# Turning token rows through DRAM and VectorE's 32x32 transposition instead of TensorE, and longer rests in one gating group

## The chip, the cores and the metric

The kernel runs on one core of one Trainium2 chip. The metric is the device time of one execution in microseconds; less is better. A profiled execution also gives a trace, with a span a little shorter than its time.

## The reference

Sliding-window attention feeds a dense feed-forward layer, and that a mixture of eight experts, of which each token uses two:

```python
# attention: 4 batches, 8 heads, 576 positions, head size 64, window 64
mask = (rel >= 0) & (rel < window)
out = softmax(where(mask, scale * q @ k.T, -1e9)) @ v        # -> x, 2304 tokens x 512
# dense layer
h = maximum(x @ w_in, 0)                                     # 512 -> 2048
x = h * h @ w_out                                            # 2048 -> 512
# mixture
noisy = x @ w_gate + log1p(exp(x @ w_noise)) * noise         # 2304 x 8
top2, top2_w = two largest of each row, softmax over the two
for e in range(8):
    for k in range(2):
        m = top2[:, k] == e
        out[m] += top2_w[m, k, None] * (maximum(x[m] @ w1[e], 0) @ w2[e])   # 512 -> 1024 -> 512
```

All of it is float32. The kernel holds each operand of the large matrix products as a pair (high part, rest), and makes three products out of each.

## The kernel before

The 2304 tokens are worked on in six groups g of 384, three tiles of 128 each. For each group PE makes the dense layer over 16 slices f of the hidden width: L1 (L329) gives a slice of h, L2 (L346) adds it to three PSUM accumulators named o. At a group's end the three tiles are copied into SBUF buffers x2 and written to the DRAM tensor x2d (L375). Three more streams are Python generators, from which a function `filler` takes a step here and there between L1 and L2: the attention of group g + 1, the gating of group g - 1, and later the preparation of the next expert's tokens.

The gating of a group needs the tokens with their 512 features on partitions. Four PE transpositions a tile (L387) put a tile into a PSUM bank named att, ScalarE copies it out as the high part (L390), VectorE subtracts for the rest (L391). Eight matmuls (L396) give the logits; a long chain of small VectorE operations finds the two experts of each token, and small matmuls with the triangle `tri` and with `ones` (L457 to L459) count places. Ahead of these, and of the last one of the gating (L501), stand REST = 4 empty yields, so that filling work lies in between while VectorE ends its chain.

Then come nine expert passes: expert 0 in two (three tiles, two tiles), experts 1 to 7 in one pass each of five tiles, at most 624 tokens. In a pass, f runs over 8 slices of the hidden width. Its L1 runs in two halves of 312 columns, each into one of the two PSUM banks h; ScalarE takes the relu (L582), VectorE the rest h (L583), and then the bank is free. `stage2` loads the two weight tiles st2 of the next expert's slice f by two DMAs of 256 KB on SP (L533, L535), from four buffers, and splits them on ScalarE (L148) and POOL (L149). `prep`, begun at f = 4 of each pass, gathers the next expert's token rows from x2d into gx0 to gx4 by indirect DMA on POOL (L546), turns each tile by four PE transpositions (L564), and copies and subtracts as in the gating (L566, L567). At the end of a pass `finish` gathers the rows of out (gy), adds into buffers y, and scatters them (L552).

The generators only give the order in which the program is written. A list scheduler, which knows costs and dependences, then puts the instructions of each engine into an order of its own, and each engine works strictly in that order. DMAs issued by SP take turns over eight lanes, and each waits for the one eight before it.

Of the kernel before, what the change touches and what calls it, by code (L numbers as in the profile page):

```python
# [8 lines left out]
F32 = mybir.dt.float32  # L9
# [4 lines left out]
AF = mybir.ActivationFunctionType  # L14
OP = mybir.AluOpType
AX = mybir.AxisListType
REST = 4
NREST = 1
P0F = 6
PNF = 4  # L20
LB = 4
QB = 0
KT = 1
# [17 lines left out]
def moe_kernel(ctx, tc, q, k, v, w_in, w_out, wg, wn, noise, w1, w2, out):  # L41
    nc = tc.nc
    B, H, S, D = q.shape
    N, DM = out.shape
    E, _, F2 = w1.shape
    F = w_out.shape[0]
    NCC = DM // 128
# [3 lines left out]
    TG = 384  # L51
    TT = TG // 128
    NG = N // TG
# [6 lines left out]
    CT = -(-CAP // 128)  # L60
# [6 lines left out]
    hw = ctx.enter_context(tc.tile_pool(name="hw", bufs=2))  # L67
    xtp = ctx.enter_context(tc.tile_pool(name="xtp", bufs=2))
    ringa = ctx.enter_context(tc.tile_pool(name="ringa", bufs=2 * NF2))
    att = tc.alloc_tile_pool(name="att", bufs=2, side="right")  # L70
# [4 lines left out]
    dram = ctx.enter_context(tc.tile_pool(name="dram", bufs=1, space=DRAM))  # L75
# [6 lines left out]
    def ps(tag):  # L82
        return psum.tile([128, 512], F32, name=tag, tag=tag, bufs={"o": 3, "h": 2, "att": 3}[tag])
# [37 lines left out]
    def late_consts():  # L121
        nc.gpsimd.iota(iotas, pattern=[[1, 128]], base=0, channel_multiplier=0,
                       allow_small_or_imprecise_dtypes=True)
        nc.gpsimd.iota(pidx, pattern=[[0, 1]], base=0, channel_multiplier=1,
                       allow_small_or_imprecise_dtypes=True)
        nc.gpsimd.memset(ones, 1.0)
        nc.gpsimd.affine_select(out=tri, in_=ones, pattern=[[1, 128]], compare_op=OP.is_gt,
                                fill=0.0, base=0, channel_multiplier=-1)
        nc.gpsimd.memset(base, 0.0)
        nc.gpsimd.memset(cnt, 0.0)  # L130
        nc.gpsimd.memset(table, 0.0)
        wf = stg.tile([128, 512], F32, name="cv", bufs=CVB)[:, :NCC * 2 * E].rearrange("p (c e) -> p c e", c=NCC)
        nc.sync.dma_start(wf[:, :, :E], wg.rearrange("(c p) e -> p c e", p=128))
        nc.sync.dma_start(wf[:, :, E:], wn.rearrange("(c p) e -> p c e", p=128))
        nc.scalar.activation(wgn[:, :, 0], wf, AF.Copy)
        nc.gpsimd.tensor_sub(wgn[:, :, 1], wf, wgn[:, :, 0].bitcast(F32))
        nt = stg.tile([N // 128, 128 * E], F32, name="st", bufs=STB)
        nc.sync.dma_start(nt, noise.rearrange("(t p) e -> t (p e)", p=128))
        pn = ps("att")
        for e in range(E):  # L140
            nc.tensor.transpose(pn[:, e * (N // 128):(e + 1) * (N // 128)],
                                nt.rearrange("t (p e) -> t e p", e=E)[:, e], ident[:N // 128, :N // 128])
        nc.vector.tensor_copy(noi.rearrange("p t e -> p e t"),
                              pn[:, :N // 128 * E].rearrange("p (e t) -> p e t", e=E))
# [231 lines left out]
                x2s[g].append(x2)  # L376


    GAT = {}

    def gating(g):
        gat = GAT["pool"]
        x2T = gat.tile([128, 2, NCC, TG], F32R, name="x2T")
        for t in range(TT):
            pt = ps("att")
            for c in range(NCC):
                nc.tensor.transpose(pt[:, 128 * c:128 * c + 128], x2s[g][t][:, 128 * c:128 * c + 128], ident)  # L387
            tl = slice(128 * t, 128 * t + 128)
            src = pt.rearrange("p (c n) -> p c n", c=NCC)
            nc.scalar.activation(x2T[:, 0, :, tl], src, AF.Copy)  # L390
            nc.vector.tensor_sub(x2T[:, 1, :, tl], src, x2T[:, 0, :, tl].bitcast(F32))  # L391
            yield
        pl = ps("att")
        for c in range(NCC):
            for i in range(2):
# [54 lines left out]
        V.memset(cm[:, 0, 0], 0.0)  # L450
        for t in range(TT):
            V.tensor_add(cm[:, t + 1, 0], cm[:, t, 0], cm[:, t, 1])
        for _ in range(REST):
            yield
        pc = ps("att")
        nE = TT * E
# [37 lines left out]
                             bc(tok[:, TT * g:TT * g + TT], NS))  # L494
        for c, val in ((1, wh.bitcast(F32)), (2, wl)):
            nc.gpsimd.tensor_mul(Bv[:, :, :, c], Bo, bc(val, NS))
        for _ in range(REST):
            yield
        pk = ps("att")
        for i in range(2 * TT):  # L500
# [29 lines left out]
    def stage2(e, f):  # L530
        pool = M2["stg"]
        st = pool.tile([128, 1024], F32, name="st2")
        nc.sync.dma_start(st[:, :512].rearrange("p (c f) -> p c f", c=NCC),  # L533
                          w1[e, :, 128 * f:128 * f + 128].rearrange("(c p) f -> p c f", p=128))
        nc.sync.dma_start(st[:, 512:], w2[e, 128 * f:128 * f + 128, :])  # L535
        ws = []
        for i in range(2):
            w = ringa.tile([128, 2, 512], F32R, name="w")
            split(w, st[:, 512 * i:512 * i + 512], nc.gpsimd)
            ws.append(w)  # L540
        return ws
# [3 lines left out]
    def gather(dst, src, i):  # L545
        nc.gpsimd.indirect_dma_start(  # L546
            out=dst, out_offset=None, in_=src[:, :],
            in_offset=bass.IndirectOffsetOnAxis(ap=slot[i][0][:dst.shape[0]], axis=0),
            bounds_check=N - 1, oob_is_err=False)
# [6 lines left out]
    def prep(tiles, xT):  # L556
        for j, i in enumerate(tiles):
            gather(gx[j], x2d, i)
        for _ in range(NREST if len(tiles) == 2 else 0):
            yield  # L560
        for j, i in enumerate(tiles):
            pt = ps("att")
            for c in range(NCC):
                nc.tensor.transpose(pt[:, 128 * c:128 * c + 128], gx[j][:, 128 * c:128 * c + 128], ident)  # L564
            src = pt.rearrange("p (c n) -> p c n", c=NCC)
            nc.scalar.activation(xT[:, 0, :, 128 * j:128 * j + 128], src, AF.Copy)  # L566
            nc.vector.tensor_sub(xT[:, 1, :, 128 * j:128 * j + 128], src,  # L567
                                 xT[:, 0, :, 128 * j:128 * j + 128].bitcast(F32))
            yield

    w2s = {}
# [57 lines left out]
    def add_fill(gen, n):  # L629
        fill.append(gen)  # L630
        left[0] += n
# [50 lines left out]
    for g in range(NG):  # L682
        drain()
        if g == 1:
            stg.release()
            GAT["pool"] = tc.alloc_tile_pool(name="gat", bufs=1)
        if g == NG - 1:
            att.release()
            gxp = tc.alloc_tile_pool(name="gxp", bufs=1, side="right")
            gx = []  # L690
            for j in range(CT):
                t = gxp.tile([128, DM], F32, name=f"gx{j}")
                nc.vector.memset(t, 0.0)
                gx.append(t)
            M2["stg"] = tc.alloc_tile_pool(name="stg2", bufs=2, side="right")
        if g + 1 < NG:
            add_fill(att_group(g + 1), 4 * UG)
        for f in range(NF):
            if g == NG - 1 and f >= 2 and f - 2 < NF2:
                w2s[0, f - 2] = stage2(0, f - 2)  # L700
            if g == 0 and f == NF - 3:
                late_consts()
            if g == 1 and f == 8:
                clear_out()
            slots = 2 * (NF - f)
            L1(g, f)
            filler(-(-left[0] // slots))
            if prev:
                L2(*prev)
            if f == 0 and g > 0:  # L710
                add_fill(gating(g - 1), 6 + 2 * REST)
            if f == NF - 1 and g == NG - 1:
                drain()
                index_tables(0, TT)
                xA = xtp.tile([128, 2, NCC, TG], F32R, name="xT")
                add_fill(prep(list(range(TT)), xA), TT)
            filler(-(-left[0] // (slots - 1)))
            prev = (g, f)
# [10 lines left out]
    for n, (e, tiles) in enumerate(passes):  # L729
# [15 lines left out]
        for f in range(NF2 + 1):  # L745
            if f < NF2:
                h = m2_L1(e, f, T, xcur)
            filler(1)
            if f == (P0F if n == 0 else PNF) and n == 0:
                drain()  # L750
                index_tables(TT, NS)
            pending += [(hprev, w2s[e, f - 1][1])] if f else []
            if pending and not (n + 1 == len(passes) and f == NF2 - 1):
                if o is None:
                    o = [ps("o" if j < 3 else "att") for j in range(len(tiles))]
                accumulate(o, pending, f == 1, f == NF2)
                pending = []
                filler(1)
            hprev = h

            if n >= 1 and f < NF2 and e + 1 < E:
                w2s[e + 1, f] = stage2(e + 1, f)
            if f == (P0F if n == 0 else PNF) and n + 1 < len(passes):
                nt = passes[n + 1][1]
                if n == 0:
                    xnext = xtp.tile([128, 2, NCC, 256], F32R, name="xT")
                else:
                    xnext = M2["x"].tile([128, 2, NCC, 128 * CT], F32R, name="x2T2")
                add_fill(prep(nt, xnext), len(nt))
        drain()  # L770
        if e > 0 and not gy:
            for j in range(CT):
# [22 lines left out]
    with tc.For_i(0, more['n']):  # L795
# [44 lines left out]
        pt = ps("att")  # L840
# [48 lines left out]
```

## Time and profile before

| | |
|---|---|
| median of three runs | 1043.31 us (1041.99 to 1045.19) |
| profiled execution | 1041.95 us, span 1040.2 us |
| PE busy | 1015.1 us (98%) |
| VectorE, ScalarE, POOL busy | 47%, 40%, 33% of the span |
| granted PE clock, mean | 0.994 of full speed |

PE is TensorE's matmul side and PEld its weight loads, DVE is VectorE, ACT is ScalarE, POOL is GpSimd, SP issues most DMAs. The groups of rows below come from the page and from views of the trace; a line L329 is a line of the kernel as printed above.

### The profile page before, as it was taken

What the parts mean: (1) busy time and instruction counts of PE and PEld (TensorE: products, weight loads), DVE (VectorE), ACT (ScalarE), POOL (GpSimd) and SP (SyncE); (2) the same over time, 40 slices, a digit from 0 to 9 for tenths busy, and PEclk for the clock granted to TensorE, in tenths of its full rate; (3) what the DMA queues carried; (4) which work ended last, traced back from release to release, by engine and by line L of the source; (5) the groups of instructions that cost most, each with busy time, mean ns of one, the idle gap of its engine ahead of it and who ended that gap; (6) DMA issues with size and microseconds to landing.
All of it is one profiled execution on the core that took longest, in us unless ns stands there. A gap on an engine that the chain in (4) does not pass through costs nothing.

```text
span 1040.2 us, 16792 instructions
## 1 busy us (share of the span) xinstructions
PE 1015.1 (98%) x6120; PEld 896.5 (86%) x6120; DVE 486.7 (47%) x1243; ACT 420.7 (40%) x1037; POOL 346.8 (33%) x357
## 2 busy tenths in 40 slices
PE   7988999999999999999899999999999999999997
PEld 6766788888889888888799889989988999899896
DVE  7999976447436544744743622131313122231312
ACT  4776654435335444443432244333323332333210
POOL 3110101002000110100350067756655756565411
PEclk9999999999999999999999999999999999999999
DMA  9756573121112113112320345544443434343111
GB/s 203 210 182 179 141 237 94 28 74 33 43 38 66 40 28 80 35 23 60 109 71 9 104 130 186 169 130 129 145 139 117 152 120 155 120 139 107 46 48 49
DMA packets 148737, 108.34 MB, mean 104 GB/s; under 512 B 85753, under 2 KB 126713, under 8 KB 148651
## 3 DMA queue, kind: packets, MB, share of 16 engines
q1 hardware_dynamic: 139451, 80.09, 27.1%
q0 software_dynamic: 9200, 27.14, 8.1%
q8 instruction: 50, 0.82, 0.3%
q14 instruction: 36, 0.29, 0.1%
HBM read 89.27 MB, written 20.48 MB: 106 GB/s over the span
## 4 chain that ended last, share of the span: by engine, by line
PE 80%; DVE 7%; issue 5%; DMA 4%; ACT 2%; POOL 1%; POOLq 0%; SPq 0%; ACTq 0%; DVEq 0%
PE h L329 35%; PE o L346 28%; PE att L346 6%; PE att L283 2%; PE att L255 2%; PE att L564 2%; DMA st<-in_moe_w_in_dram 1%; PE att L272 1%; DVE w L149 1%; DMA st<-in_moe_w_out_dram 1%; PE att L396 1%; DVE x L162 1%; PE att L387 1%; PE att L236 1%; POOL out_dram L552 1%
## 5 line engine op out<-in xcount | busy, mean ns | idle before, releaser
L346 PE MATMUL o<-w,h 128*128 128x512 f32 x1488 | 393.5, 401 | 3.6 <-ACT w L148 2.3
L346 PEld LDWEIGHTS o<-w,h 128*128 128x128 f32 x1488 | 269.9, 189 | 59.7 <-ACT w L148 4.6
L329 PE MATMUL h<-xT,w 128*128 128x384 f32 (+1 forms) x1344 | 261.8, 341 | 2.9 <-DVE r L356 2.6
L329 PEld LDWEIGHTS h<-xT,w 128*128 128x128 f32 x1344 | 228.9, 190 | 9.3 <-DVE r L356 3.5
L329 PE MATMUL h<-x2T,w 128*128 128x312 f32 x1344 | 201.4, 307 | 0.0
L149 POOL TENSOR_TENSOR w<-st,w 128x512 fp32r<-128x512 f32 x128 | 164.8, 1298 | 105.6 <-ACT w L148 84.4
L329 PEld LDWEIGHTS h<-x2T,w 128*128 128x128 f32 x1344 | 195.8, 188 | 3.6
L583 DVE SCALAR_TENSOR_TENSOR h<-h 128x312 fp32r<-128x312 f32 (+2 forms) x128 | 61.9, 483 | 272.2 <-ACT h L582 272.2
L148 ACT ACTIVATE w<-st 128x512 fp32r<-128x512 f32 x128 | 80.8, 631 | 191.3 <-PE att L346 120.0
L268 POOL TENSOR_TENSOR P<-P,stat 128x384 f32<-128x384 f32 x48 | 42.3, 883 | 263.1 <-DVE stat L267 126.5
L354 ACT ACTIVATE r<-h 128x384 f32<-128x384 f32 x96 | 46.8, 487 | 145.2 <-PE h L329 139.1
L582 ACT ACTIVATE h<-h 128x312 fp32r<-128x312 f32 (+2 forms) x128 | 54.4, 425 | 116.5 <-PE h L329 116.5
L346 PE MATMUL att<-w,h 128*128 128x512 f32 (+1 forms) x336 | 94.3, 393 | 0.0
L356 DVE TENSOR_TENSOR r<-h,r 128x384 f32<-128x384 f32 x96 | 53.1, 553 | 76.5 <-ACT h L355 75.1
L346 PEld LDWEIGHTS att<-w,h 128*128 128x128 f32 (+1 forms) x336 | 61.0, 181 | 15.4
L546 POOL DMA_INDIRECT gx<-x2d,ix x40 | 40.9, 1022 | 49.6 <-PE att L564 41.2
L357 DVE TENSOR_TENSOR h<-r,h 128x384 fp32r<-128x384 f32 x96 | 55.9, 582 | 2.7
L355 ACT ACTIVATE h<-r 128x384 fp32r<-128x384 f32 x96 | 50.2, 523 | 1.6
L552 POOL DMA_INDIRECT out_dram<-y,ix x35 | 34.5, 984 | 44.1 <-DVE y L594 37.0
L265 ACT ACTIVATE P<-P,stat 128x128 f32<-128x128 f32 x96 | 37.6, 392 | 25.3 <-DVE stat L263 20.7
L546 POOL DMA_INDIRECT gy<-out_dram,ix x35 | 35.6, 1017 | 19.3 <-issue 19.0
L567 DVE TENSOR_TENSOR x2T<-att,x2T 128x512 fp32r<-128x512 f32 x35 | 24.2, 691 | 36.2 <-ACT x2T L566 35.9
(207 smaller groups left out, 921.2 us busy)
## 6 DMA issues: line engine op xcount, KB each, us to landing
st<-in_moe_w_dram SPq DMA_DIRECT2D x128, 256.0 KB, 3.0
st<-in_moe_w_in_dram SPq DMA_DIRECT2D x16, 512.0 KB, 4.8
st<-in_moe_w_out_dram SPq DMA_DIRECT2D x16, 512.0 KB, 3.7
vn<-in_v_dram SPq DMA_DIRECT2D x110, 64.0 KB, 2.3
x2d<-x SPq DMA_DIRECT2D x18, 256.0 KB, 3.3
out_dram<-x SPq DMA_DIRECT2D x1, 4608.0 KB
qn<-in_q_dram SPq DMA_DIRECT2D x40, 96.0 KB, 2.5
kn<-in_k_dram SPq DMA_DIRECT2D x28, 128.0 KB, 2.8
```

The costliest lines, as they stand in the source:

```text
L148: nc.scalar.activation(dst[:, 0], src, AF.Copy)
L149: engine.tensor_sub(dst[:, 1], src, dst[:, 0].bitcast(F32))
L329: nc.tensor.matmul(p[:, :n], w[:, wi, 128 * c:128 * c + 128], x[:, xi, c], start=(c == 0 and i == 0), stop=(c == NCC - 1 and i == 2))
L346: nc.tensor.matmul(o[t][:hs.shape[1]], hs, w[:, wi], start=(first and i == 0 and hi == 0 and wi == 0), stop=(last and i == len(steps) - 1 ...
L354: nc.scalar.activation(r, ph[:, :TG], AF.Relu)
L355: nc.scalar.activation(h[:, 0], r, AF.Square)
L356: nc.vector.tensor_mul(r, ph[:, :TG], r)
L357: nc.vector.tensor_sub(h[:, 1], r, h[:, 0].bitcast(F32))
L546: nc.gpsimd.indirect_dma_start(out=dst, out_offset=None, in_=src[:, :], in_offset=bass.IndirectOffsetOnAxis(ap=slot[i][0][:dst.shape[0]], ...
L552: return nc.gpsimd.indirect_dma_start(out=out[:, :], out_offset=bass.IndirectOffsetOnAxis(ap=slot[i][0][:src.shape[0]], axis=0), in_=src, ...
L582: nc.scalar.activation(h[:, 0, a:a + m], ph[:, :m], AF.Relu)
L583: nc.vector.scalar_tensor_tensor(h[:, 1, a:a + m], ph[:, :m], 0.0, h[:, 0, a:a + m].bitcast(F32), op0=OP.max, op1=OP.subtract)
```

## The change

For the gating of groups 0 to 3 (12 tiles) and the preparation of experts 2 to 7 (30 tiles) the transposition leaves PE. A tile's rows are read from DRAM by four DMAs of 64 KB in pieces of 512 bytes, each DMA to 32 partitions, so that the four blocks of features and the four blocks of tokens already stand in their places; VectorE's transposition of 32x32 blocks does the rest, into a PSUM bank att, and the copy and the subtraction follow as before. In the gating the rows are x2d's; for an expert the gathered tiles are first written to a DRAM tensor xg. The feature order becomes d = 4p + c, so the gating weights and those of experts above 1 are loaded in that order, and the PE transpositions that remain in the gating (groups 4 and 5) read every fourth column. The preparation of experts 2 to 7 begins at f = 1 instead of 4. Group 4's two rests are 8 yields instead of 4.

```diff
+PTF = 1
-        nc.sync.dma_start(wf[:, :, :E], wg.rearrange("(c p) e -> p c e", p=128))
-        nc.sync.dma_start(wf[:, :, E:], wn.rearrange("(c p) e -> p c e", p=128))
+        nc.sync.dma_start(wf[:, :, :E], wg.rearrange("(p c) e -> p c e", p=128))
+        nc.sync.dma_start(wf[:, :, E:], wn.rearrange("(p c) e -> p c e", p=128))
...
+    def turned_rows(raw, src, row):
+        for a in range(4):
+            nc.sync.dma_start(raw[32 * a:32 * a + 32].rearrange("p (q d) -> p q d", q=4),
+                              src[row:row + 128, 128 * a:128 * a + 128].rearrange("(q i) d -> i q d", i=32))
+
+    def turn(xT, raw):
+        tmp = ps("att")
+        nc.vector.transpose(tmp.rearrange("p (c q i) -> p q c i", c=NCC, q=4),
+                            raw.rearrange("p (q j c) -> p q c j", q=4, c=NCC))
+        src = tmp.rearrange("p (c n) -> p c n", c=NCC)
+        nc.scalar.activation(xT[:, 0], src, AF.Copy)
+        nc.vector.tensor_sub(xT[:, 1], src, xT[:, 0].bitcast(F32))
...
     def gating(g):
         gat = GAT["pool"]
         x2T = gat.tile([128, 2, NCC, TG], F32R, name="x2T")
...
+        rest = REST if g != NG - 2 else 2 * REST
+        if g < NG - 2:
+            raws = [hw.tile([128, DM], F32, name="x2", bufs=3) for _ in range(TT)]
+            for t, raw in enumerate(raws):
+                turned_rows(raw, x2d, TG * g + 128 * t)
+            for _ in range(3):
+                yield
+            for t, raw in enumerate(raws):
+                turn(x2T[:, :, :, 128 * t:128 * t + 128], raw)
+                yield
+        else:
+            for t in range(TT):
+                pt = ps("att")
+                for c in range(NCC):
+                    nc.tensor.transpose(pt[:, 128 * c:128 * c + 128], x2s[g][t][:, c::NCC], ident)
...
-        for _ in range(REST):
+        for _ in range(rest):
             yield
...
         nc.sync.dma_start(st[:, :512].rearrange("p (c f) -> p c f", c=NCC),
-                          w1[e, :, 128 * f:128 * f + 128].rearrange("(c p) f -> p c f", p=128))
+                          w1[e, :, 128 * f:128 * f + 128].rearrange("(p c) f -> p c f" if e > 1 else "(c p) f -> p c f",
+                                                                    p=128))
...
+    def prep_turned(tiles, xT):
+
+        for j, i in enumerate(tiles):
+            gather(gx[j], x2d, i)
+        for _ in range(3):
+            yield
+        xg = dram.tile([128 * len(tiles), DM], F32, name="xg", bufs=2)
+        raws = [hp2.tile([128, DM], F32, name="y", bufs=CT) for _ in tiles]
+        for j in range(len(tiles)):
+            nc.sync.dma_start(xg[128 * j:128 * j + 128, :], gx[j])
+        for _ in range(2):
+            yield
+        for j, raw in enumerate(raws):
+            turned_rows(raw, xg, 128 * j)
+        for _ in range(2):
+            yield
+        for j, raw in enumerate(raws):
+            turn(xT[:, :, :, 128 * j:128 * j + 128], raw)
             yield
...
-                add_fill(gating(g - 1), 6 + 2 * REST)
+                add_fill(gating(g - 1), 9 + 2 * REST if g < NG - 1 else 6 + 4 * REST)
...
-            if f == (P0F if n == 0 else PNF) and n + 1 < len(passes):
+            if f == (P0F, PNF, PTF)[min(n, 2)] and n + 1 < len(passes):
...
-                add_fill(prep(nt, xnext), len(nt))
+                add_fill((prep_turned if n > 1 else prep)(nt, xnext), len(nt) + (7 if n > 1 else 0))
```

The scheduler's orders move by this. VectorE in the pass of expert 2, as it was: the names are the result and the operands, h is the rest of a half of L1's slice, two rows for each f, and the rows begin with f = 0.

```order
L583 SCALAR_TENSOR_TENSOR h_7498<-h_7499,h_7498 128x312
L583 SCALAR_TENSOR_TENSOR h_7498<-h_7514,h_7498 128x312
L583 SCALAR_TENSOR_TENSOR h_7538<-h_7539,h_7538 128x312
L583 SCALAR_TENSOR_TENSOR h_7538<-h_7554,h_7538 128x312
L583 SCALAR_TENSOR_TENSOR h_7598<-h_7599,h_7598 128x312
L583 SCALAR_TENSOR_TENSOR h_7598<-h_7614,h_7598 128x312
```

And as it is with the change, at the same place (y is the tile read back, att the PSUM bank):

```order
L631 SCALAR_TENSOR_TENSOR h_7538<-h_7539,h_7538 128x312
L631 SCALAR_TENSOR_TENSOR h_7538<-h_7554,h_7538 128x312
L631 SCALAR_TENSOR_TENSOR h_7578<-h_7579,h_7578 128x312
L631 SCALAR_TENSOR_TENSOR h_7578<-h_7594,h_7578 128x312
L388 STREAM_TRANSPOSE att_7896<-y_7756 128x4x4x32
L392 TENSOR_TENSOR x2T2_7638<-att_7896,x2T2_7638 128x4x128
L388 STREAM_TRANSPOSE att_7940<-y_7757 128x4x4x32
L392 TENSOR_TENSOR x2T2_7638<-att_7940,x2T2_7638 128x4x128
L631 SCALAR_TENSOR_TENSOR h_7639<-h_7640,h_7639 128x312
L388 STREAM_TRANSPOSE att_7959<-y_7758 128x4x4x32
L631 SCALAR_TENSOR_TENSOR h_7639<-h_7655,h_7639 128x312
```

Two transpositions with their subtractions have come between the rows of f = 1 and the first of f = 2; the passes of expert 1 and of experts 3 to 6 have the same.

POOL in the pass of expert 1, behind the gathers of gy, as it was (w is the rest of a weight split, st2 the loaded tile, gx the gathered rows of an expert):

```order
L149 TENSOR_TENSOR w_7123<-st2_7120,w_7123 128x512
L149 TENSOR_TENSOR w_7126<-st2_7120,w_7126 128x512
L149 TENSOR_TENSOR w_7178<-st2_7175,w_7178 128x512
L546 DMA gx0_5500<-x2d_81,ix3_6507 128x512
L149 TENSOR_TENSOR w_7181<-st2_7175,w_7181 128x512
L546 DMA gx1_5502<-x2d_81,ix3_6507 128x512
L149 TENSOR_TENSOR w_7263<-st2_7260,w_7263 128x512
L546 DMA gx2_5504<-x2d_81,ix3_6507 128x512
```

And with the change:

```order
L150 TENSOR_TENSOR w_7111<-st2_7105,w_7111 128x512
L574 DMA gx0_5524<-x2d_81,ix3_6531 128x512
L150 TENSOR_TENSOR w_7174<-st2_7171,w_7174 128x512
L574 DMA gx1_5526<-x2d_81,ix3_6531 128x512
L574 DMA gx2_5528<-x2d_81,ix3_6531 128x512
L574 DMA gx3_5530<-x2d_81,ix3_6531 128x512
L150 TENSOR_TENSOR w_7177<-st2_7171,w_7177 128x512
L574 DMA gx4_5532<-x2d_81,ix3_6531 128x512
L574 DMA gx0_5524<-x2d_81,ix3_6531 128x512
L150 TENSOR_TENSOR w_7249<-st2_7246,w_7249 128x512
L574 DMA gx1_5526<-x2d_81,ix3_6531 128x512
```

Before, one expert's five gathers stood in this pass; now those of four experts (and two left over) do, ahead of expert 1's scatters.

SP at the beginning of the pass of expert 2, as it was, held weight loads alone:

```order
L533 DMA st2_7391<-in_moe2_w1_dram 128x4x128
L535 DMA st2_7391<-in_moe2_w2_dram 128x512
L533 DMA st2_7529<-in_moe2_w1_dram 128x4x128
L535 DMA st2_7529<-in_moe2_w2_dram 128x512
```

With the change (xg are the gathered rows in DRAM):

```order
L560 DMA st2_7700<-in_moe2_w1_dram 128x4x128
L563 DMA st2_7700<-in_moe2_w2_dram 128x512
L608 DMA xg_9967<-gx3_5530 128x512
L608 DMA xg_9967<-gx4_5532 128x512
L383 DMA y_7756<-xg_7755 32x4x128 x2
L560 DMA st2_7766<-in_moe2_w1_dram 128x4x128
L563 DMA st2_7766<-in_moe2_w2_dram 128x512
L383 DMA y_7756<-xg_7755 32x4x128 x2
L383 DMA y_7757<-xg_7755 32x4x128 x4
```

The first tile's four reads now have a weight load in their middle, and 16 more reads follow.

## Rows read from the trace of the kernel before

**Rows 1.** The page: span, and busy us (share) xinstructions of each engine

```profile
span 1040.2 us, 16792 instructions
PE 1015.1 (98%) x6120; PEld 896.5 (86%) x6120; DVE 486.7 (47%) x1243; ACT 420.7 (40%) x1037; POOL 346.8 (33%) x357
```

**Rows 2.** Groups by line and shape: xcount | busy us, mean ns | idle before

```profile
L564 PE MATMUL att<-ident,gx 128*128 128x128 f32 x160 | 23.6, 272 | 0.2 <-DMA gx<-x2d,ix 0.2
```

**Rows 3.** Chain of waits around group 4's gating: start, us on the chain, piece

```profile
493.63 0.44 PE att L387 x4
...
517.01 4.05 PE h L329 x12
521.06 2.99 PE o L346 x9
524.06 2.10 PE h L329 x12
526.16 2.08 PE o L346 x9
```

**Rows 4.** Timeline of PE, group 4: start, us, instruction [idle before <-releaser]

```profile
515.24 0.19 PE L457 MATMUL att<-cm,tri 128*128 128x24 bf16 x1 [1.51 <-DVE cm L449]
516.65 0.18 PE L458 MATMUL att<-cm,ones 128*128 128x24 bf16 x1 [1.23 <-DVE cm L452]
```

**Rows 5.** Windows: us, PE, PEld, DVE, ACT, POOL busy, PEclk, DMA share, GB/s

```profile
515.00:520.00 5.00, 3.52 (x13) 3.37 (x14) 4.60 (x23) 0.00 (x0) 1.38 (x2) 0.61 0.36 107
640.00:660.00 20.00, 20.00 (x115) 17.98 (x114) 2.63 (x6) 6.05 (x12) 14.65 (x14) 1.00 0.49 160
```

**Rows 6.** Groups by line and shape, VectorE and ScalarE

```profile
L566 ACT ACTIVATE x2T<-att 128x512 fp32r<-128x512 f32 x35 | 20.5, 586 | 0.0
L567 DVE TENSOR_TENSOR x2T<-att,x2T 128x512 fp32r<-128x512 f32 x35 | 24.2, 691 | 36.2 <-ACT x2T L566 35.9
L161 DVE SCALAR_TENSOR_TENSOR x<-st,x 128x512 int32<-128x512 int32 x24 | 17.3, 723 | 0.0
L583 DVE SCALAR_TENSOR_TENSOR h<-h 128x312 fp32r<-128x312 f32 x112 | 54.0, 482 | 250.1 <-ACT h L582 250.1
```

**Rows 7.** DMA issues: xcount, KB each, us to landing; last row within 560 to 600

```profile
st<-in_moe_w_dram SPq DMA_DIRECT2D x128, 256.0 KB, 3.0
vn<-in_v_dram SPq DMA_DIRECT2D x110, 64.0 KB, 2.3
x2d<-x SPq DMA_DIRECT2D x18, 256.0 KB, 3.3
out_dram<-y,ix POOLq DMA_INDIRECT x35, 2.7
...
st<-in_moe_w_dram SPq DMA_DIRECT2D x8, 256.0 KB, 5.2
```

**Rows 8.** Timeline of PE: L1 of f = 3 in the passes of experts 1, 2, 3

```profile
650.53 3.59 PE L329 MATMUL h<-x2T,w 128*128 128x312 f32 x24
...
708.00 3.59 PE L329 MATMUL h<-x2T,w 128*128 128x312 f32 x24
...
765.37 3.59 PE L329 MATMUL h<-x2T,w 128*128 128x312 f32 x24
```

**Rows 9.** Timeline of POOL, passes of experts 1 and 3

```profile
642.82 1.31 POOL L149 TENSOR_TENSOR w<-st,w 128x512 fp32r<-128x512 f32 x1
644.30 1.01 POOL L552 DMA_INDIRECT out_dram<-x,ix  x1 [0.17 <-issue]
649.29 1.05 POOL L546 DMA_INDIRECT gy<-out_dram,ix  x1 [3.98 <-issue]
...
747.05 1.02 POOL L552 DMA_INDIRECT out_dram<-y,ix  x1 [0.16 <-DVE y L594]
```

**Rows 10.** Timeline of SP's queue: start, us, DMA

```profile
217.86 4.72 SPq L204 DMA_DIRECT2D vn<-in_v_dram  x6
...
644.15 0.38 SPq L533 DMA_DIRECT2D st<-in_moe_w_dram  x1
644.57 0.51 SPq L535 DMA_DIRECT2D st<-in_moe_w_dram  x1
```

More of the change, by code (lines that the diff above doesn't have):

```diff
@@ L383, in gating @@
         x2T = gat.tile([128, 2, NCC, TG], F32R, name="x2T")
[L384 to L392, printed above, removed]
+        rest = REST if g != NG - 2 else 2 * REST
[13 more added lines that the diff above has]
+                    nc.tensor.transpose(pt[:, 128 * c:128 * c + 128], x2s[g][t][:, c::NCC], ident)
+                tl = slice(128 * t, 128 * t + 128)
+                src = pt.rearrange("p (c n) -> p c n", c=NCC)
+                nc.scalar.activation(x2T[:, 0, :, tl], src, AF.Copy)
+                nc.vector.tensor_sub(x2T[:, 1, :, tl], src, x2T[:, 0, :, tl].bitcast(F32))
+                yield
         pl = ps("att")
@@ L496, in gating @@
             nc.gpsimd.tensor_mul(Bv[:, :, :, c], Bo, bc(val, NS))
-        for _ in range(REST):
+        for _ in range(rest):
             yield
@@ L568, in prep @@
                                  xT[:, 0, :, 128 * j:128 * j + 128].bitcast(F32))
+            yield
[9 more added lines that the diff above has]
+        for _ in range(2):
+            yield
+        for j, raw in enumerate(raws):
+            turned_rows(raw, xg, 128 * j)
+        for _ in range(2):
+            yield
+        for j, raw in enumerate(raws):
+            turn(xT[:, :, :, 128 * j:128 * j + 128], raw)
             yield
```

## Prediction

> **What bounds the kernel now.** I read the page's busy shares first: TensorE works 1015.1 of 1040.2 us, the next engine under half of that [rows 1]. So what counts is whether PE has an instruction less, or waits for one. From the groups by line I took what one transposition costs [rows 2], from the chain of waits what it is worth on the path [rows 3], from the timelines where PE waits in group 4 [rows 4] and how late data may come in the expert passes [rows 8 to 10].
>
> The sum is made against the profiled execution, 1041.95 us; the median of the three runs is 1.36 us above it, and that is added at the end.
>
> **Removed: 168 PE transpositions.** Of a tile's four, 0.44 us stands on the chain [rows 3]. 12 gating tiles give 5.3 us, 30 expert tiles 13.2 us. An upper bound is the group's busy time, 23.6 us over 160 or 0.59 a tile [rows 2], so 24.8 instead of 18.5.
>
> **Moved: the rests of group 4.** PE waits 1.51 us for the first matmul of its prefix sums and 1.23 for the second [rows 4], both for VectorE's chain; behind that it has run at a granted clock of 0.61 [rows 5], between its two levels, and twelve L1 products take 4.05 instead of 2.10 us, nine L2 products 2.99 instead of 2.08 [rows 3]. Four more yields put four fillings of about 2.1 us ahead of the two matmuls, and VectorE has ended 1.2 us after the first was reached. The gain is 1.51 + 1.23 + 1.95 + 0.91 = 5.6 us; it would be less only if the instructions behind come too late, and the next consumer, the gating of group 5, is tens of us away. Together with the transpositions: 24.1 us gained.
>
> **Added: 42 VectorE transpositions (T).** No row has one. The nearest are 128x512 instructions of VectorE: a subtraction that reads PSUM 0.691, an int32 operation that reads every second word 0.723 [rows 6]. I take 0.7; as bounds 0.48, which one of 312 columns takes [rows 6], and twice 0.65, 1.3 (rival C). Then come the ScalarE copy, 0.59, and the subtraction, 0.69 [rows 6], as before. VectorE is 47% busy [rows 1], so the 29 us themselves fit beside PE; only their place in its order can cost.
>
> **Added: 48 reads in the gating.** x2d is written at the end of a group (3.3 us to landing) and read by 64 KB pieces; pieces of that size land after 2.3 us [rows 7], and each costs SP 0.79 us (4.72 over six) [rows 10], so twelve take 9.4 us. Three yields and the scheduler's place for T cover most of this: it moved the eight logits matmuls about one and a half f later, into the products of L1 at f = 4. But there they stand between products, and PE cannot pass them. Lower bound 0 a group; upper, that one whole T, copy and subtraction (2.0 us) lies open; nearer to the first, as the matmuls were moved with it: 0.75. Four groups: 3 us (0 to 8).
>
> **Added: the way of experts 2 to 7 through DRAM.** Here the order matters. In every pass from expert 1 on, T0 stands on VectorE behind the four h subtractions of f = 0 and 1, and T1 behind it, both ahead of the one for the first half of f = 2. L1 of f = 3 needs the PSUM bank that this one reads. So whenever T0's data come late, PE stops at the start of f = 3: 650.53 in the pass of expert 1, 708.00 in that of expert 2, 765.37 in that of expert 3 [rows 8]. From T0's data to that bank free: T, copy, subtraction, twice, then 0.48 for h: 2 x (0.7 + 0.59 + 0.69) + 0.48 = 4.4 us.
>
> *Pass of expert 1.* Three more gathers stand ahead of the POOL split that frees the buffer of the weight load before the last two reads of tile 0. The split ends at 644.13 before [rows 9]; with 3 x 1.3 (a gather is 1.0 and 0.3 between) 648.0. SP then issues that load, 0.38 + 0.51, and two reads at about 0.5 each: 649.9; landing 2.3 [rows 7]: 652.2; plus 4.4: 656.6. PE wants it at 650.53: a stall of 6.1. After an interruption of 2.7 us in group 4 PE paid 2.86 us at the lower clock (above), so I add 2.9: 9.0 us.
>
> *Pass of expert 2.* Tile 0's read goes into a y buffer that expert 1's first scatter must have left, and its last two reads stand on SP behind a weight load whose buffer is freed by the split after four scatters. POOL now has 42 instructions (27 gathers, 15 splits) between the last scatter of expert 0 and the first of expert 1, as all gathers of experts 4 to 7 were drawn into this stretch. Expert 0's last scatter ends at 645.3 [rows 9], now 649.2; the wait of 3.98 us before the first gather back [rows 9] moves with it to 653.2; 41 instructions at 1.3 us give 706.5; four scatters and the split 713.0; load and two reads 1.9: 714.9; landing 2.3, then 4.4: 721.6. Also 20 tiles of 256 KB are gathered and written in this stretch, 10 MB beside the weights, so landing can be long: 5.2 us instead of 3.0 was seen for weight loads in the busiest stretch [rows 7]. I add 3 (0 to 10): 724.6. PE comes to f = 3 at 708.0 + 9.0 - 2.2 (five tiles without transposition) = 714.8. Stall 9.8, with the clock 12.7.
>
> *Passes of experts 3 to 6.* All gathers are past, POOL has slack. Expert 2's first scatter begins at 747.05 [rows 9] and lands 2.7 after its 1.0 us [rows 7]: 750.8. Tiles 0 and 1 need eight reads and one load on SP, 5.7 us at 0.6 a read, and 2.3 to land: 758.8; T, copy, subtraction and h, 2.5: 761.3, against 765.37 [rows 8]. A margin of 4 us, so no stall.
>
> Losses: 3 + 9.0 + 12.7 = 24.7 against 24.1. The change gives back what it gains: 1041.95 + 0.6 + 1.36 = 1044 us. Group 4's and 5's 24 transpositions now read x with a step of 16 bytes as stationary operand; I take nothing: weight loads, 896.5 us over 6120 [rows 1] or 0.15 each, lie beside matmuls.
>
> **Rivals.**
> *A, the waits at T0 don't reach PE* (.27). If POOL's extra gathers wait for nothing and fit into its idle time, T0 comes before f = 3. For it: POOL is busy a third of the span [rows 1]. Against: from 640 to 660 it already works 14.65 of 20 us [rows 5]. Without either stall the time is 1043.3 - 24.1 + 3 = 1022; with one of them 1031 to 1035.
>
> *B, every pass stalls* (.15; slower). Place: the reads of tiles 0 and 1 in the passes of experts 2 to 6. Price of a read at 0.79 us on SP [rows 10] and a landing of 5.2 [rows 7]: 750.8 + 7.2 + 5.2 + 2.5 = 765.7, which is past 765.37. From there each pass pays the excess and 2.9 for the clock. An excess of 1 in four passes is 16 us: 1060; of 3, 1068. For it: 20 reads with 512-byte pieces are a new kind of traffic. Against: before, the DMA engines were busy to 0.49 in an expert pass [rows 5].
>
> *C, strided reads cost double* (.10; slower). T reads its tile with a step of 16 bytes. Then T is 1.3: 0.6 more for each tile in the gating that lies open (two of three, four groups: 4.8), 1.2 in each of the two stalls, and 24 transpositions at 0.15 more (3.6 us). Sum 10.8: 1055. Against: the read of every second word costs 0.723 where the subtraction costs 0.691 [rows 6], but that is a step of 8 bytes.
>
> [...]
>
> **How the numbers follow.** The main case, stalls of some 22 us in the passes of experts 1 and 2 against a gain of 24, has .48, and a range of its own of 1034 to 1054: the busy-time bound of the transpositions (-6), the gating (-3 to +5), landing (-3 to +7). What this kernel's measurement can tell from no change is about 0.3%, 3 us. Of the main case faster gets .13, same .21, slower .14; of A .24 and .03; B is slower; of C .08 slower, .02 same. That makes faster .37, same .26, slower .37. The range from A to B leaves out A's lowest and B's highest: 1023 to 1059.
>
> **What would show it.** In the profile after: PE idle before L1 of f = 3 in the passes of experts 1 and 2, put down to VectorE's h and behind it T's reads; POOL solid from 650 to 713; no such wait from expert 3 on; no idle time at the tri and ones matmuls of group 4 and a granted clock of 1.0 behind it; T near 0.7. The forecast is wrong if PE runs through f = 3 in both passes (A), if the waits repeat five times (B), or if T is over 1.0 (C).

## The result, and the profile after

The changed kernel took 1058.85 us (1055.96 to 1059.68, four runs) beside 1043.32 for the kernel before: a ratio of 1.0131, 95% interval 1.0113 to 1.0149. So the change is slower by 1.3%. The forecast was 1044, with chances of .37 for faster, .26 for the same and .37 for slower; the time lies 0.15 us under the upper end of the range, 1059.

PE is busy 13.5 us less, and for a smaller share, as the page says (compare [rows 1]):

```profile
span 1056.8 us, 16806 instructions
PE 1001.6 (95%) x5952; PEld 881.2 (83%) x5952; DVE 527.4 (50%) x1285; ACT 422.1 (40%) x1037; POOL 345.9 (33%) x357
```

The list of what PE waited for (us in total, times, longest) begins with a wait that it did not have before, twice in the program, and has a single wait of 3.0 us without a named releaser ("issue"):

```profile
PE h L330 <- DVE h L631: 25.0, 2, 19.6
PE o L347 <- ACT w L149: 4.0, 6, 1.1
PE o L347 <- issue: 3.0, 1, 3.0
```

The timeline of PE has the first two at the start of f = 3 in the passes of experts 1 and 2, the places of [rows 8], and the third, called the stop below, in expert 0's second pass. From expert 3 on f = 3 has no wait. In group 4's gating the wait ahead of the first prefix-sum matmul is gone:

```profile
522.08 0.19 PE L484 MATMUL att<-cm,tri 128*128 128x24 bf16 x1
...
609.00 2.93 PE L347 MATMUL o<-w,h 128*128 128x512 f32 x6 [3.04 <-issue]
...
656.43 4.99 PE L330 MATMUL h<-x2T,w 128*128 128x312 f32 x24 [5.42 <-DVE h L631]
...
732.75 5.98 PE L330 MATMUL h<-x2T,w 128*128 128x312 f32 x24 [19.58 <-DVE h L631]
...
790.31 3.59 PE L330 MATMUL h<-x2T,w 128*128 128x312 f32 x24
```

The stop stands behind ScalarE. Its relu of the first slice, which L2 needs, began at 608.56, 5.6 us after PE had begun L1 of that slice; in a second profile of the same program (e8 below) it began 1.6 us after. What held ScalarE the trace does not name ("remote"):

```profile
608.56 0.38 ACT L630 ACTIVATE h<-h 128x256 fp32r<-128x256 f32 x1 [3.63 <-remote]
```

On VectorE the two waits stand in front of T0, and the h subtraction of f = 2 is behind it (L631 at 655.91 and 732.23). The last row is the same subtraction in the pass of expert 3:

```profile
651.05 1.10 DVE L388 STREAM_TRANSPOSE att<-y 128x512 f32<-128x512 f32 x1 [8.85 <-DMA y<-xg]
652.82 0.69 DVE L392 TENSOR_TENSOR x2T<-att,x2T 128x512 fp32r<-128x512 f32 x1 [0.66 <-ACT x2T L391]
653.55 1.09 DVE L388 STREAM_TRANSPOSE att<-y 128x512 f32<-128x512 f32 x1
655.30 0.69 DVE L392 TENSOR_TENSOR x2T<-att,x2T 128x512 fp32r<-128x512 f32 x1 [0.66 <-ACT x2T L391]
655.91 0.47 DVE L631 SCALAR_TENSOR_TENSOR h<-h 128x312 fp32r<-128x312 f32 x1
...
727.39 1.09 DVE L388 STREAM_TRANSPOSE att<-y 128x512 f32<-128x512 f32 x1 [23.03 <-DMA y<-xg]
...
732.23 0.47 DVE L631 SCALAR_TENSOR_TENSOR h<-h 128x312 fp32r<-128x312 f32 x1
...
788.63 0.47 DVE L631 SCALAR_TENSOR_TENSOR h<-h 128x312 fp32r<-128x312 f32 x1
```

On POOL the gathers of four experts stand in the pass of expert 1 (the flood, below), and the first scatter of expert 1 comes at 714.66. Five times a gather also waits, some 2 us each, for an earlier write to xg to have read its buffer:

```profile
651.89 1.05 POOL L574 DMA_INDIRECT gy<-out_dram,ix  x1 [0.16 <-issue]
...
669.30 1.01 POOL L574 DMA_INDIRECT gx<-x2d,ix  x1 [2.26 <-DMA xg<-gx]
...
673.51 1.01 POOL L574 DMA_INDIRECT gx<-x2d,ix  x1 [1.88 <-DMA xg<-gx]
...
686.29 1.00 POOL L574 DMA_INDIRECT gx<-x2d,ix  x1 [2.26 <-DMA xg<-gx]
...
697.20 1.01 POOL L574 DMA_INDIRECT gx<-x2d,ix  x1 [2.17 <-DMA xg<-gx]
...
708.33 1.01 POOL L574 DMA_INDIRECT gx<-x2d,ix  x1 [2.35 <-DMA xg<-gx]
...
714.66 1.02 POOL L580 DMA_INDIRECT out_dram<-y,ix  x1 [0.17 <-issue]
```

In the kernel before, the first scatter of expert 1 came 25 us earlier:

```profile
689.66 1.03 POOL L552 DMA_INDIRECT out_dram<-y,ix  x1
```

To see where the time goes, the same matmuls of the dense layer's and the experts' L1 are set beside each other in the two timelines of PE. The table gives after minus before, in us, for the profiled execution of the change and for that of e8; a minus means that PE is ahead of the kernel before:

| up to | after | e8 | term of the prediction |
|---|---|---|---|
| start of group 1 | -0.4 | -0.6 | none (start) |
| start of group 5 | -1.2 | -1.4 | gating: -5.3 + 3 |
| expert 0's second pass | -5.7 | -6.0 | rests: -5.6 |
| start of expert 1's pass | +0.3 | -6.0 | none |
| f = 4 of expert 1's pass | +7.3 | +5.3 | stall +9.0 |
| start of expert 2's pass | +5.0 | +3.0 | five tiles -2.2 |
| f = 4 of expert 2's pass | +27.2 | +25.5 | stall +12.7 |
| f = 4 of expert 7's pass | +15.9 | +14.2 | 25 tiles -11 |

### The profile page after: what moved, and what is told of

It reads as the page before. It is cut to its first block, busy times and chain, and to the rows that moved or that the text cites. A ratio compares the mean times of both kernels' runs of the same rounds, so it can differ in the third digit from the quotient of the medians.

```text
span 1056.8 us, 16806 instructions
## 1 busy us (share of the span) xinstructions
PE 1001.6 (95%) x5952; PEld 881.2 (83%) x5952; DVE 527.4 (50%) x1285; ACT 422.1 (40%) x1037; POOL 345.9 (33%) x357
## 4 chain that ended last, share of the span: by engine, by line
PE 64%; DVE 10%; issue 9%; DMA 6%; POOL 5%; SPq 2%; ACT 2%; POOLq 1%; DVEq 0%; ACTq 0%
PE h L330 28%; PE o L347 23%; PE att L347 5%; POOL w L150 3%; PE att L284 2%; DMA xg<-gx 2%; PE att L256 2%; SPq L383 1%; POOL gx L574 1%; DVE w L150 1%; DMA st<-in_moe_w_in_dram 1%; PE att L273 1%; DVE att L388 1%; POOL out_dram L580 1%; PE att L423 1%
## 5 line engine op out<-in xcount | busy, mean ns | idle before, releaser
L330 PE MATMUL h<-x2T,w 128*128 128x312 f32 x1344 | 204.2, 309 | 25.0 <-DVE h L631 25.0
L330 PEld LDWEIGHTS h<-x2T,w 128*128 128x128 f32 x1344 | 200.2, 192 | 30.5 <-DVE h L631 25.9
L631 DVE SCALAR_TENSOR_TENSOR h<-h 128x312 fp32r<-128x312 f32 (+2 forms) x128 | 61.6, 481 | 239.3 <-ACT h L630 205.4
L391 ACT ACTIVATE x2T<-att 128x512 fp32r<-128x512 f32 x42 | 25.1, 597 | 89.5 <-DVE att L388 79.1
L388 DVE STREAM_TRANSPOSE att<-y 128x512 f32<-128x512 f32 x30 | 33.1, 1104 | 41.7 <-DMA y<-xg 41.3
L266 ACT ACTIVATE P<-P,stat 128x128 f32<-128x128 f32 x96 | 37.6, 392 | 23.6 <-DVE stat L264 23.6
```

The source lines that it names most:

```text
L330: nc.tensor.matmul(p[:, :n], w[:, wi, 128 * c:128 * c + 128], x[:, xi, c], start=(c == 0 and i == 0), stop=(c == NCC - 1 and i == 2))
L631: nc.vector.scalar_tensor_tensor(h[:, 1, a:a + m], ph[:, :m], 0.0, h[:, 0, a:a + m].bitcast(F32), op0=OP.max, op1=OP.subtract)
```

## The experiments

Ratios are to the kernel before on the same chip, run in turn with it.

**The change once more (e8).**

> The changed kernel once more, as a yardstick beside the others. The stalls of 5.4 and 19.6 us should come again to within 1 us. Open is the stop of PE for 3 us in the pass of expert 0's last two tiles, for which the trace names no releaser and which none of the four kernels before this showed: if it belongs to the order of this program, it is there again at the same place; if it is chance, the span is 6 us shorter, 1051.

1056.39 us, ratio 1.0145 (1.0129 to 1.0162). The stop in expert 0's second pass is gone, yet the span is only 1.3 us shorter and not 6: the first stall is now 9.44 us and not 5.42, so that it did not come again to within 1 us.

```profile
654.15 5.29 PE L330 MATMUL h<-x2T,w 128*128 128x312 f32 x24 [9.44 <-DVE h L631]
731.04 6.02 PE L330 MATMUL h<-x2T,w 128*128 128x312 f32 x24 [19.87 <-DVE h L631]
```

PE came to f = 3 of expert 1 6.3 us earlier than in the first profile and went on only 2.3 us earlier: the data of T0, which POOL and SP bring, follow PE's time only in part. The stop of 3 us had used up part of a wait that was due anyway. Its cause stays open: the profile of none of the ten runs e1 to e10 has it. The sizes of the terms below are therefore read from e8.

**The rests alone (e1)**: in the kernel before, `REST if g != NG - 2 else 2 * REST` in both loops and `6 + 4 * REST` in the filler's count for the gating of group 4.

> The kernel before with group 4's longer rests alone. From the two traces, the rests are worth 5.3 us (the lead of the changed kernel at L1 grows from 1.2 to 6.5 us there): about 1038 us. The changed kernel then loses 6.0 us in the pass of expert 0's last two tiles, where its PE stands still for 3 us without a wait that the profile can name. If that loss comes with the shift of PE's work in time, it shows here too, and the time is 1043 to 1044; if it comes with the turned rows, it does not.

1037.05 us, ratio 0.9967 (0.9954 to 0.9979), faster by 3.4 us in the median. In its timeline PE's lead over the kernel before grows by 4.7 us, from 1.9 at the start of group 5 to 6.6 at expert 0's second pass. No stop there.

**Gating and rests without the experts' part (e4)**:

```diff
-            if f == (P0F, PNF, PTF)[min(n, 2)] and n + 1 < len(passes):
+            if f == (P0F if n == 0 else PNF) and n + 1 < len(passes):
...
-                add_fill((prep_turned if n > 1 else prep)(nt, xnext), len(nt) + (7 if n > 1 else 0))
+                add_fill(prep(nt, xnext), len(nt))
```

and w1 loaded as before for all experts.

> The changed kernel with all experts' rows turned by PE as before: left of the change are the gating of groups 0 to 3 by VectorE and the longer rests. Theory: 1.2 + 5.3 us of gain, no stall at f = 3: about 1037 us, or 1043 if the 6 us loss in the pass of expert 0's last two tiles is there too, which would bind it to the gating or the rests; if it is not there it belongs to the experts' part. Rival for the gating: turning it gains the 5.3 us of its 48 transpositions, then 1033.

1036.08 us, ratio 0.9958 (0.9944 to 0.9972). No stall and no stop. So what makes the change slower is in the experts' part, and the rest of it gains. The rival for the gating, 1033, did not come.

**Only the gathers held back (e2)**:

```diff
-        for j, i in enumerate(tiles):
-            gather(gx[j], x2d, i)
+        last = next(x for x in reversed(nc.cur_bb.bb.instructions) if x.engine == mybir.EngineType.Pool)
+        with tc.issue_after(last):
+            for j, i in enumerate(tiles):
+                gather(gx[j], x2d, i)
```

> The changed kernel, with the gathers of experts 2 to 7 queued on POOL behind the work that was written before them, so that only one expert's gathers stand in a pass. Theory: the two stalls at f = 3 (5.4 and 19.6 us, with the clock 7.0 and 22.1) come from the flood of gathers in the pass of expert 1, through the scatters that it delays and through T's early place, which follows from the early gathers. Then both stalls go, and 1.2 (gating), 5.3 (rests) and 13.5 us (experts) are left of the gain: 1023 us, or 1029 if the 6 us loss before them stays. Rival: the way through DRAM is too long for a pass anyway; then each of six passes has a stall at the T's, and the time stays above 1040.

1070.93 us, ratio 1.0298 (1.0280 to 1.0316): slower than the change. The theory as I had put it fell. Without the flood the two long stalls are gone, but there is a shorter one in each of six passes. The scheduler had moved T0 only to between the two subtractions of f = 4, and the data were 8 us later than that:

```profile
PE h L330 <- DVE h L633: 33.9, 6, 6.1
```

```profile
716.19 0.48 DVE L633 SCALAR_TENSOR_TENSOR h<-h 128x312 fp32r<-128x312 f32 x1 [4.11 <-ACT h L632]
724.89 1.09 DVE L388 STREAM_TRANSPOSE att<-y 128x512 f32<-128x512 f32 x1 [8.22 <-DMA y<-xg]
```

Its five gathers begin at 711.11, and T0 at 724.89: gather, write, read and landing take 14 us when no gather waits on POOL. The rival forecast the outcome, a stall in each of six passes and a time above 1040. Its reason, a way through DRAM too long for a pass, does not hold: e5 below has the same way and no stall.

**Only the transpositions held back (e3)**: `tc.keep_in_program_order` on each T of the experts, so that T0 stands behind the subtractions of f = 5; the flood stays.

> The changed kernel with the flood of gathers left as it is, but with each VectorE transposition of an expert queued behind what was written before it on VectorE, so that they stand behind the h subtractions of f = 5 and later instead of those of f = 1. Theory: what stops PE is T's place ahead of the h subtraction of f = 2; then both stalls go although POOL, its scatters and the reads are as late as in the changed kernel, and the time is 1023 to 1029 us. Rival: POOL's lateness itself is what PE ends up waiting for (weight splits, y); then POOL's order costs 10 us or more elsewhere, and the time is above 1035.

1043.25 us, ratio 1.0027 (1.0017 to 1.0037): 1% better than the change, and on the rival's side, above 1035. No T stands ahead of the subtractions of f = 2 any more. Four of the five waits that are left (12.5 of 13.7 us) are a second way in which the flood reaches PE, in the pass of expert 2, and there ScalarE is late with the relu:

```profile
PE h L330 <- DVE h L633: 13.7, 5, 5.4
```

```profile
704.83 0.63 ACT L149 ACTIVATE w<-st 128x512 fp32r<-128x512 f32 x1 [10.20 <-DMA st<-in_moe_w_dram]
705.37 0.41 ACT L632 ACTIVATE h<-h 128x312 fp32r<-128x312 f32 x1
```

A weight load waits for the buffer that a late POOL split frees (in e8, with the same flood, one goes out at 699.08, the split having ended at 699.06); ScalarE stands at the next split for that load (10.20 us above), with the relu behind it, and then the h subtraction. So the rival was right for that pass.

**Both held back (e5)**: the two edits together.

> The changed kernel with both queues held: the gathers of an expert as in e2_gathers_kept, and its VectorE transpositions as in e3_turns_kept. With the gathers held alone, the first tile's data came about 35 us after the pass began, and T0 stood between the two h subtractions of f = 4: six stalls of 5 to 6 us. Theory: the way through DRAM is longer than the scheduler reckons, and all that matters for PE is whether an h subtraction stands behind a T whose data are not there. Held behind f = 5, T0 comes when its data are there: no stall, 6.6 us gained before the experts and 13.5 in them, 20 us below the kernel before on the same chip. Rival: the five tiles then end too late for the next pass; PE waits at each pass's start, and less than 10 us are gained.

1023.25 us, ratio 0.9830 (0.9816 to 0.9845). No wait of the experts' L1 for h is left, and T0 starts without idle time; it is 17.4 us below the kernel before, where 20 were expected:

```profile
719.08 0.48 DVE L635 SCALAR_TENSOR_TENSOR h<-h 128x312 fp32r<-128x312 f32 x1 [2.08 <-ACT h L634]
719.48 1.09 DVE L388 STREAM_TRANSPOSE att<-y 128x512 f32<-128x512 f32 x1
```

The same computation, DMAs and transpositions as the change, 33 us faster (against e8, on the same chip) by order alone. A second run of it (e10) gave 1022.83 us, ratio 0.9834 (0.9818 to 0.9850).

**Own buffers for the tiles read back (e7)**:

```diff
-        raws = [hp2.tile([128, DM], F32, name="y", bufs=CT) for _ in tiles]
+        raws = [hp2.tile([128, DM], F32, name="raw", bufs=2) for _ in tiles]
```

> The changed kernel, where the tiles read back have two buffers of their own instead of the five y buffers, so that the reads of the first two tiles need not wait for the scatters of the expert before. The order of VectorE and the flood of gathers stay. Theory: in the pass of expert 2 the reads wait for the scatters, which POOL issues 24 us later than before, behind the gathers; then the stall of 19.6 us falls to under 5, and the time by 17 us or more, to about that of the kernel before. Rival: the traffic of the stretch (the DMA engines are busy to 0.87) makes the reads late by itself; then a stall of over 10 us stays.

1096.16 us, ratio 1.0527 (1.0510 to 1.0544). The time came out far from the theory's, and a stall of over 10 us stays, as the rival had it, but not for its reason. T0 and T1 answer the question: free of the y buffers, their reads went out from 674.83 on, in the pass of expert 1, and in the pass of expert 2 the two run without a wait. The DMA engines moved as much then (220 GB/s from 658 to 685 and 263 from 685 to 712, two slices of the page) as at the end of the change's long wait (224 GB/s from 720 to 728); so it was the scatters that had held them, and not the traffic. But there are only two such buffers, and T2's reads stand on SP behind a weight load that waits for a split on POOL (it goes out at 734.45, the split having ended at 734.42), so the same stall (19.32 us) moves to T2, ahead of the second subtraction of f = 2. The pass of expert 1 now stalls twice (9.45 and 7.03 us), and later passes stall too (four waits, 23.6 us together).

```profile
712.57 1.09 DVE L388 STREAM_TRANSPOSE att<-raw 128x512 f32<-128x512 f32 x1
...
740.98 1.09 DVE L388 STREAM_TRANSPOSE att<-raw 128x512 f32<-128x512 f32 x1 [23.07 <-DMA raw<-xg]
```

**T without the step of 16 bytes (e6)**: `raw.rearrange("p (q c j) -> p q c j", ...)` for the experts' 30 T.

> The changed kernel, where the 30 VectorE transpositions of experts 2 to 7 read their tile in its order in memory instead of with a step of 16 bytes; the features then come out in a wrong order, so that the experts' products are of other numbers, with all work as before. The 12 of the gating keep the step and stand beside them. T took 1.10 us in the changed kernel. If the step costs it (rival C of the prediction), the 30 take about 0.7 and the 12 stay at 1.1; if the transposition itself is slow, all take 1.1. PE's time moves by under 2 us in either case.

One run, 1055.18 us. The groups by line and shape part as rival C has it:

```profile
L388 DVE STREAM_TRANSPOSE att<-y 128x512 f32<-128x512 f32 x30 | 21.7, 724 | 47.8 <-DMA y<-xg 47.4
L388 DVE STREAM_TRANSPOSE att<-x 128x512 f32<-128x512 f32 x12 | 13.4, 1115 | 0.4 <-DMA x<-x2d 0.4
```

Its span, 1053.5 us, is 2.0 below e8's, whose stalls it keeps (8.29 and 18.55 us). One execution, beside two profiles of the changed kernel that lie 1.3 us apart, does not make a price of this.

**The gating back on PE (e9)**, and e5 again (e10) beside it: e5 with PE's transpositions in the gating of all groups.

> e5_both_kept with the gating of all groups turned by PE as before, and its weights in their old order; the rests of group 4 and the experts' part stay. In the changed kernel each turned group gains about 1.3 us by three tiles without transpositions and loses most of it in the next, where in three groups PE waits 0.7 to 0.85 us for ScalarE at the logits matmuls; 0.2 to 1.3 us of gain were left of it over four groups. Theory: the gating's part is worth about 1 us, so this kernel is 0 to 2 us slower than e5_both_kept beside it. Rival: its 48 reads and transpositions cost as much as they bring, then the two agree or this one is faster.

> e5_both_kept once more, as the yardstick for e9_gating_on_pe on the same chip. It should again be 1.7% faster than the kernel before, with no wait for T's data on PE.

1023.24 and 1022.83 us, ratios 0.9837 (0.9820 to 0.9854) and 0.9834: no difference that can be told. A gain of 0.8 us by the gating, as the timelines have it, is too small to show.

## Why it came out so

**The mechanism was the forecast one.** Two stalls at f = 3, in the passes of experts 1 and 2 and in no later one, with T0 waiting for its reads and the h subtraction of f = 2 behind it. e2, e3 and e5 show that it takes an order on two engines, the flood on POOL and T's early place on VectorE: with the flood alone mended 33.9 us of waits at L1 stay, with T's place alone 13.7, with both none. Two of the signs that the prediction named did not come: T took 1.10 us and not about 0.7, and POOL was not solid from 650 to 713 but waited between its gathers.

**That the time lies in the range is luck.** The main case, which came about, had a range of its own of 1034 to 1054, and 1058.85 is outside it. The whole range reached to 1059 for the sake of rival B, which did not occur.

**What failed was the size of the second stall**, first in the step "41 instructions at 1.3 us give 706.5". The gathers did not follow each other at 1.3 us: five times they waited 1.9 to 2.4 us for the write to xg that still read their buffer, where 0.3 was reckoned. The scatter came at 714.66 (713.75 in e8). With T at 1.10 us instead of 0.7, twice, PE went on at 732.75 (731.04 in e8) and not at 724.6. And PE came to f = 3 at 711.17 in e8, and not at 714.8. It lost 22.5 us there in e8, where the prediction had 12.7.

**The first stall** cost 11.3 us in e8, where 9.0 was forecast: 9.44 of wait, and the rest behind it at a granted clock that had fallen during the wait (0.59 in the mean of 646 to 654), where the first products took 5.29 us instead of 3.59. In the profiled execution of the change the clock was 0.50 from 656 to 659, behind the same wait, and 1.00 from 660 on. The prediction took the times of PE (650.53) and of POOL's split (644.13) from the kernel before, as if the gains ahead of this pass moved neither. In e8 PE was at f = 3 at 644.71, 5.8 us earlier, and went on at 654.15, only 2.4 us before the forecast 656.6. In the profiled execution the stop hid part of the stall: 6.0 + 7.0 there, 0 + 11.3 in e8, 1.7 us apart. That PE went on there at 656.43, so near the forecast, is luck too: the split ended 3.0 us earlier than reckoned (644.96), T0 began 6.1 us behind it and not 4.2, and from T0 to PE it took 5.4 us and not 4.4.

**The gains** came near the forecast for the experts and the rests, and short of it in the gating: 13.6 us in the experts (13.2 forecast; 2.2 to 2.3 a pass in e8, where five times 0.44 is 2.2), 4.6 by the rests (5.6 forecast; of a lead that rises by 5.3, 0.7 is given back within the next slices), 0.8 by the gating (2.3 forecast, too small to show in e9 beside e10). In the gating each group gains about 1.3 us and loses about 1.1: in three groups the logits matmuls, now inside L1, wait for ScalarE's copy of PT:

```profile
244.81 0.36 PE L423 MATMUL att<-x2T,wgn 128*32 128x384 f32 x1 [0.85 <-ACT PT L278]
333.52 0.36 PE L423 MATMUL att<-x2T,wgn 128*32 128x384 f32 x1 [0.68 <-ACT PT L278]
```

Added up for e8: -0.6 - 0.8 - 4.6 + 11.3 + 22.5 - 13.6 = 14.2 us, as the table has it up to f = 4 of expert 7's pass; the prediction's own terms gave 0.6. The sum was off by 13.6, of which 12.1 are the two stalls.

**The rivals.** A did not occur in the change; e5 comes near what it described (21 us below the kernel before; e5 is 17.4 below). B did not occur in the change, but its margin was thin: in expert 3's pass the h subtraction ended at 789.10 and PE took the bank at 790.31, 1.2 us where the prediction had 4. With the gathers held alone (e2) every pass did stall, but behind f = 4 and not by B's price of the reads: there a read took SP 0.48 us (9.14 over 19) and landed in 2.0, where B had 0.79 and 5.2. C was right that the step costs time: T costs 1.10 us with the step and 0.72 without (e6), past the 1.0 that the prediction had named as a sign against itself, and the 24 strided transpositions' weight loads cost 204 ns, beside 141 for the others and 140 at the same place before. That the step doubles them, 1.3 us for a T and 0.15 more for a weight load, was C's guess, and no run shows it: it was 0.38 us more on T and 63 ns on a weight load. C's price is shown only in part. Of its 10.8 us, 2.4 were for T in the two stalls; e6, which takes the step out there alone, came out 2.0 us below e8 in one execution. The weight loads cost 24 times 63 ns, or 1.5 us beside the matmuls, and not 3.6 on the path: on the chain of waits a tile's four transpositions take 0.47 us, where they took 0.44. What T's step costs in the gating no run takes apart.

```profile
L592 PEld LDWEIGHTS att<-ident,gx 128*128 128x128 f32 x40 | 4.7, 141 | 1.0 <-PE att L592 0.5
L414 PEld LDWEIGHTS att<-ident,x 128*128 128x128 f32 x24 | 3.7, 204 | 0.2
```

And before, with the columns in order:

```profile
L387 PEld LDWEIGHTS att<-ident,x 128*128 128x128 f32 x72 | 8.6, 140 | 0.5
```

## What to carry to other kernels

Work that is taken off the bounding engine and sent through memory pays or costs by the order on the other engines (here 1023.25 us or 1056.39): ask of each in-order queue which instruction stands behind the one that now waits, and how long the bounding engine does without it. When a scheduler draws early-ready instructions forward, look at what they displace, and count the waits between them too (here a buffer that an earlier write still reads). A wait whose end depends on other engines swallows delays ahead of it (here 4 of 6.3 us), and gains ahead of it too, so a stall's length in one trace is not its price, and its start and end are not both read from the trace before.

## What was not expected of the hardware

A step of 16 bytes cost VectorE's transposition half as much again (1.10 us against 0.72 in e6) and PE's weight load 45% (204 against 141 ns). And PE stopped once for 3.04 us behind a relu of ScalarE that began 4 us late with no releaser in the trace, in one profile of the two of this program; what it was stays open.
